# Second MLP: the normalised tile is turned in 32x32 blocks on VectorE and by DMA through DRAM instead of on TensorE

## The chip, the cores and the metric

One core of a Trainium2 chip. The metric is the device time of one execution in microseconds; a kernel's time is the median of its runs. A core has TensorE (PE, with its weight loads shown as PEld), VectorE (DVE), ScalarE (ACT), GpSimd (POOL) and SyncE (SP), whose queue issues nearly all DMAs here.

## What is computed

Memory attention, then two MLPs over 4352 tokens of 512 features (`S` = 512 tokens and 32 state rows for each of 8 batches). The change touches the second MLP alone:

```python
def _moe2_ref(x, w_in, w_out, g_ln):           # w_in 512 x 1024, w_out 1024 x 512
    h = x @ w_in
    e = np.exp(h - np.max(h, axis=-1, keepdims=True))
    sm = e / (np.sum(e, axis=-1, keepdims=True) + 1e-09)
    solu = h * sm
    mu = np.mean(solu, axis=-1, keepdims=True)
    var = np.mean((solu - mu) ** 2, axis=-1, keepdims=True)
    ln = (solu - mu) / np.sqrt(var + 1e-06) * g_ln
    return (ln @ w_out).astype(np.float32)
```

All matrix products keep nearly full f32 precision: each operand is split into a high part (fp32r) and the rest, and three products of the parts are summed.

## The kernel before

The first MLP writes its output, turned so that features lie on partitions, to DRAM (`x2_d`), a tensor for each block of 512 tokens and one of 256 state rows. The second MLP goes over 34 tiles of 128 tokens, four to a block and two for the state rows. A tile passes through these steps:

- `up` (line 731): 24 matmuls of 128x512, h = x W_in, into two banks of PSUM. There are two such pairs of banks (`ps_2`), used in turn, so tile s + 2 needs what tile s gave back.
- `solu_norm` (line 750): on VectorE a reduce for the maximum (752), on ScalarE the exponent with its sum (756), on VectorE the reciprocal (758) and the product with h (760), which is the last reader of the PSUM of h; on ScalarE the squares (764), on GpSimd the power -1/2 (766), on VectorE the final scale (767). The result is e, 128 tokens by 1024 features; `g_ln` is already in the weights.
- `trans` (line 770): eight TensorE transposes of 128x128 (777) into two banks, each bank then split by `split` (line 118): ScalarE copies the high part lh (119), VectorE subtracts to get ll (120).
- `down` (line 781): 24 matmuls (788 to 790) with blocks of lh and ll as the stationary operand, a copy to `ob` (801) and the store to the output (803, for state rows 808).

The loop runs over s: `up` of tile s, `down` of tile s - 2, `trans` of tile s - 1, `solu_norm` of tile s. At the end the last tile is transposed in the middle of the `down` before it. Beside this, `load_x2` (706) loads the next block from DRAM in two halves of 512 KB on SP's queue (271), and `split_x2` (714) splits them by the same `split`. In this part of the kernel the order of instructions on each engine is set by a planner from costs that it assumes; on the chip each engine takes its queue in order. Waits of DMAs stand in SP's queue and hold what is behind them.

Of the kernel before, what the change touches and what calls it, by code (L numbers as in the profile page):

```python
# [8 lines left out]
F32 = mybir.dt.float32  # L9
F32R = mybir.dt.float32r  # L10
# [10 lines left out]
def memory_attention_relu2_solu(  # L21
# [15 lines left out]
    nc = tc.nc  # L37
    P = 128
    B, H, S, D = x.shape
# [3 lines left out]
    F2 = w2_in.shape[1]  # L43
# [9 lines left out]
    NSR = B * NS  # L53
    scale = 1.0 / float(D) ** 0.5

    dram = ctx.enter_context(tc.tile_pool(name="dram", bufs=1, space=DRAM))
# [6 lines left out]
        dram.tile([P, NM, S if b < B else NSR], F32, name=f"x2_d{b}", tag=f"x2_{b}") for b in range(B + 1)  # L63
    ]

    x2p_d = [dram.tile([P, NM, S], F32, name=f"x2p_d{b}", tag=f"x2p_{b}") for b in range(2)]

    def pool(name, bufs, stack=ctx, **kw):
        return stack.enter_context(tc.tile_pool(name=name, bufs=bufs, reuse_waits="tile", **kw))
# [9 lines left out]
    swp = pool("swp", 4)  # L79
    stgp = pool("stgp", 4)  # L80
    cvp = pool("cvp", 2)
    a1p = pool("a1p", 2)
# [35 lines left out]
    def split(hi, lo, src):  # L118
        nc.scalar.activation(out=hi, in_=src, func=AF.Copy)
        nc.vector.tensor_tensor(out=lo, in0=src, in1=hi.bitcast(F32), op=ALU.subtract)  # L120
# [148 lines left out]
    def fetch32(src):  # L269
        t = stgp.tile([P, 2, 512], F32, tag="stg", name="st32")  # L270
        nc.sync.dma_start(out=t, in_=src)
        return t
# [427 lines left out]
    NK = F2 // P  # L700
# [3 lines left out]
    x2_st = {}  # L704

    def load_x2(blk):
        if blk < B:
            x2_st[blk] = [fetch32(x2_d[blk][:, 2 * i : 2 * i + 2, :]) for i in range(2)]
        else:
            t = stgp.tile([P, NM, NSR], F32, tag="stg", name="st_x2")  # L710
            nc.sync.dma_start(out=t, in_=x2_d[blk])
            x2_st[blk] = [t]

    def split_x2(blk):

        n = S if blk < B else NSR
        if blk not in x2_t:
            x2_t[blk] = (
                pools["x"].tile([P, NM, n], F32R, tag="x2h", name="x2h"),
                pools["x"].tile([P, NM, n], F32R, tag="x2l", name="x2l"),  # L720
                [],
            )
        hi, lo, at = x2_t[blk]
        st = x2_st[blk].pop(0)
        k0, nk = len(at), st.shape[1]
        at.extend(range(nk))
        split(hi[:, k0 : k0 + nk, :], lo[:, k0 : k0 + nk, :], st)
# [3 lines left out]
    def up(s, blk, t):  # L731
        xh, xl, _ = x2_t[blk]
        ps = ps_2[s % 2].tile([P, F2], F32, tag="h2", name="h2")
        for k in range(NM):
            for lt, hl in ((xh, (0, 1)), (xl, (0,))):
                for i in hl:
                    for a in range(2):
                        nc.tensor.matmul(  # L738
                            out=ps[:, a * 512 : (a + 1) * 512],
                            lhsT=lt[:, k, t * P : (t + 1) * P],  # L740
                            rhs=w2[k][:, i, a * 512 : (a + 1) * 512],
                            start=(k == 0 and lt is xh and i == 0),
                            stop=(k == NM - 1 and lt is xl),
                        )
        return ps

    def small(name):
        return pools["s"].tile([P, 1], F32, tag=name, name=name)

    def solu_norm(ps):  # L750
        nm = small("nm")
        nc.vector.tensor_reduce(out=nm, in_=ps, axis=AX.X, op=ALU.max)  # L752
        nc.vector.tensor_scalar_mul(nm, nm, -1.0)  # L753
        e = up_.tile([P, F2], F32, tag="u", name="e")
        sm = small("s2")
        nc.scalar.activation(out=e, in_=ps, func=AF.Exp, bias=nm, accum_out=sm)  # L756
        nc.vector.tensor_scalar_add(sm, sm, 1e-9)
        nc.vector.reciprocal(out=sm, in_=sm)
        mu = small("mu")
        nc.vector.scalar_tensor_tensor(out=e, in0=e, scalar=sm, in1=ps, op0=ALU.mult, op1=ALU.mult, accum_out=mu)  # L760
        nc.vector.tensor_scalar_mul(mu, mu, -1.0 / F2)  # L761
        j = evp.tile([P, F2], F32, tag="ev", name="j")
        var = small("var")
        nc.scalar.activation(out=j, in_=e, func=AF.Square, bias=mu, accum_out=var)  # L764
        nc.vector.tensor_scalar(out=var, in0=var, scalar1=1.0 / F2, scalar2=1e-6, op0=ALU.mult, op1=ALU.add)
        nc.gpsimd.tensor_tensor(out=var, in0=var, in1=mhalf, op=ALU.pow)
        nc.vector.tensor_scalar(out=e, in0=e, scalar1=mu, scalar2=var, op0=ALU.add, op1=ALU.mult)
        return e

    def trans(ln):  # L770
        lh = swp.tile([P, F2], F32R, tag="sw", name="lh")
        ll = swp.tile([P, F2], F32R, tag="sw", name="ll")
        for a in range(2):
            ps = pools["t"].tile([P, 512], F32, tag=f"t{a}", name="ps_t")
            for k in range(4):
                o = (4 * a + k) * P
                nc.tensor.transpose(ps[:, k * P : (k + 1) * P], ln[:, o : o + P], ident)  # L777
            split(lh[:, a * 512 : (a + 1) * 512], ll[:, a * 512 : (a + 1) * 512], ps)
        return lh, ll

    def down(blk, t, lh, ll, final):

        ps = pools["o"].tile([P, DM], F32, tag="o", name="ps_o")
        for k in range(NK):
            wt = w2[NM + k // 2]
            o = (k % 2) * 512
            a, bb = lh[:, k * P : (k + 1) * P], ll[:, k * P : (k + 1) * P]
            nc.tensor.matmul(out=ps, lhsT=a, rhs=wt[:, 0, o : o + 512], start=(k == 0), stop=False)  # L788
            nc.tensor.matmul(out=ps, lhsT=a, rhs=wt[:, 1, o : o + 512], start=False, stop=False)  # L789
            nc.tensor.matmul(out=ps, lhsT=bb, rhs=wt[:, 0, o : o + 512], start=False, stop=(k == NK - 1))  # L790
            yield k + 1
        ob = gp.tile([P, DM], F32, tag="gh", name="ob")
        if final:

            to = out[blk * SO : blk * SO + S].rearrange("(p t) e -> p t e", t=NT)[:, t, :]
            nc.scalar.activation(out=ob[:, : DM // 2], in_=ps[:, : DM // 2], func=AF.Copy)
            nc.vector.tensor_copy(out=ob[:, DM // 2 :], in_=ps[:, DM // 2 :])
            nc.scalar.dma_start(out=to[:, : DM // 2], in_=ob[:, : DM // 2])
            nc.sync.dma_start(out=to[:, DM // 2 :], in_=ob[:, DM // 2 :])
            return  # L800
        nc.scalar.activation(out=ob, in_=ps, func=AF.Copy)
        if blk < B:
            nc.sync.dma_start(out=out[blk * SO : blk * SO + S].rearrange("(p t) e -> p t e", t=NT)[:, t, :], in_=ob)
        else:
            per = P // NS
            for bb in range(per):
                b = t * per + bb
                nc.sync.dma_start(out=out[b * SO + S : (b + 1) * SO], in_=ob[bb * NS : (bb + 1) * NS, :])
# [30 lines left out]
    hid, sq, ready, left = {}, {}, {}, {}  # L839
# [66 lines left out]
    for s, (b, f) in enumerate(items):  # L906
# [9 lines left out]
        if g % 5 == 2 and 0 <= g // 5 + 1 < 16:  # L916
            n = g // 5 + 1
# [37 lines left out]
        n = S if b < B else NSR  # L955
# [12 lines left out]
        for e in ends.get(b, ())[1:]:  # L968
            i = f - e + 3
# [3 lines left out]
        sw = next((u for k, u in units.get(s - 2, []) if k == "i"), None)  # L973
# [26 lines left out]
    tiles = [(blk, t) for blk in [*range(B - 1), B, B - 1] for t in range(NT if blk < B else NSR // P)]  # L1000
    order = [blk for blk, t in tiles if t == 0]
# [3 lines left out]
    up_q = [solu_norm(up(0, *tiles[0]))]  # L1005
# [5 lines left out]
    ps_2[1] = pool("ps_2b", 1, space=PSUM)  # L1011
    pools["t"] = pool("ps_t", 1, space=PSUM)
    pools["o"] = pool("ps_o", 2, space=PSUM)
    ln_q = []
    for s in range(1, len(tiles) + 2):
        if s == 1:
            reload_w2(7, 1)
        if s < len(tiles):
            blk, t = tiles[s]
            i = order.index(blk) + 1  # L1020
            if i < len(order):
                if t == 0:
                    load_x2(order[i])
                if t >= 1 and x2_st[order[i]]:
                    split_x2(order[i])
                    if blk == B:
                        split_x2(order[i])
            ps = up(s, blk, t)
        if s == len(tiles) - 1:

            ln_q.append(trans(up_q.pop(0)))
        if s >= 2:
            lh, ll = ln_q.pop(0)
            for part in down(*tiles[s - 2], lh, ll, s == len(tiles) + 1):
                if s == len(tiles) and part == NK // 2:
                    ln_q.append(trans(up_q.pop(0)))
        if 1 <= s < len(tiles) - 1:
            ln_q.append(trans(up_q.pop(0)))
        if s < len(tiles):
            up_q.append(solu_norm(ps))  # L1040


# [28 lines left out]
```

## Time and profile before

| | before |
|---|---|
| median of 3 runs | 1117.78 us (1117.42 to 1118.10) |
| profiled execution, span | 1115.4 us |
| TensorE busy | 1096.8 us, 98% |
| VectorE busy | 708.5 us, 64% |
| ScalarE busy | 512.4 us, 46% |
| even part of the second MLP | 757.43 to 1075.31 us of the span, 27 tiles |

The span runs from the first to the last instruction; the time of a run lies 2.4 us above it. A timeline row gives the start from the beginning of the span, the duration, the engine, the line of the kernel, the operation, what is written and read, and in brackets the idle time before it with what ended it. Matmuls are pipelined: a row's duration is longer than the distance to the next one, so distances are read from starts.

### The profile page before, as it was taken

Reading aid. Unit: us, or ns where it says so; the run is one execution under the profiler, and the core shown is the slowest. Engines: PE = TensorE matmul, PEld = TensorE weight load, DVE = VectorE, ACT = ScalarE, POOL = GpSimd, SP = SyncE. Lnnn points to the kernel's source line nnn. Section 1 sums busy time; section 2 is a strip of 40 time slices with the busy share of each in tenths; the row PEclk is TensorE's granted clock in tenths of the full one; section 3 lists DMA queues with packets and bytes.
Section 4 is the critical chain, followed back from the end, with each engine's and each line's share of the span. In section 5 each row is a group of like instructions: output and inputs, shape, how many; then the busy total and the mean of one; then the engine's idle time right before and its main releaser. Section 6 shows DMA issues by size and latency. Waiting matters only on the chain.

```text
span 1115.4 us, 15150 instructions
## 1 busy us (share of the span) xinstructions
PE 1096.8 (98%) x5692; PEld 911.2 (82%) x5692; DVE 708.5 (64%) x1358; ACT 512.4 (46%) x903; POOL 44.7 (4%) x62
## 2 busy tenths in 40 slices
PE   5899999999999999999999999999999999999998
PEld 4788888888888888888888889888888888888887
DVE  7999995687686695884755446664545545455443
ACT  6899776455454452442333113343433334234232
POOL 1000000010000000000000000000000000000000
PEclk9899999999999999999999999999999999999999
DMA  9779883767766632412112027410101101000001
GB/s 275 253 229 311 273 276 85 239 199 221 215 198 181 200 130 69 149 62 79 40 38 76 25 91 263 151 57 20 67 19 58 67 20 41 26 20 29 20 19 38
DMA packets 93017, 134.69 MB, mean 121 GB/s; under 512 B 44816, under 2 KB 45584, under 8 KB 92944
## 3 DMA queue, kind: packets, MB, share of 16 engines
q1 hardware_dynamic: 92224, 133.46, 37.2%
q8 instruction: 45, 0.74, 0.3%
q10 hardware_dynamic: 720, 0.26, 0.1%
q14 instruction: 28, 0.23, 0.1%
HBM read 83.37 MB, written 49.28 MB: 119 GB/s over the span
## 4 chain that ended last, share of the span: by engine, by line
PE 93%; DVE 4%; ACT 1%; DMA 1%; issue 0%; ACTq 0%; POOL 0%; DVEq 0%; POOLq 0%
PE h L738 16%; PE acc L144 11%; PE acc L145 11%; PE acc L146 11%; PE ps_h L144 6%; PE ps_h L145 6%; PE ps_h L146 6%; PE ps_o L790 6%; PE ps_o L789 6%; PE ps_o L788 6%; PE ps_t L777 3%; PE ps_sr L553 2%; PE ps_x L135 1%; PE ps_sw L388 1%; PE ps_sw L389 1%; PE ps_c L494 1%
## 5 line engine op out<-in xcount | busy, mean ns | idle before, releaser
L144 PE MATMUL acc<-gh,w1out 128*128 128x512 f32 (+1 forms) x576 | 219.0, 380 | 0.0
L146 PE MATMUL acc<-gh,w1out 128*128 128x512 f32 (+1 forms) x576 | 217.9, 378 | 0.0
L145 PE MATMUL acc<-gl,w1out 128*128 128x512 f32 (+1 forms) x576 | 217.8, 378 | 0.0
L738 PE MATMUL h<-w,x2h 128*128 128x512 f32 x544 | 148.6, 395 | 0.0
L618 ACT ACTIVATE r<-ps_h 128x512 f32<-128x512 f32 (+1 forms) x144 | 82.4, 572 | 141.1 <-PE ps_h L146 139.6
L620 DVE TENSOR_TENSOR r<-r,ps_h 128x512 f32<-128x512 f32 (+1 forms) x112 | 72.4, 647 | 89.7 <-ACT r L618 89.1
L146 PEld LDWEIGHTS acc<-gh,w1out 128*128 128x128 f32 x576 | 108.4, 188 | 20.6
L144 PEld LDWEIGHTS acc<-gh,w1out 128*128 128x128 f32 x576 | 108.4, 188 | 20.4 <-DVE ev_x L657 0.2
L145 PEld LDWEIGHTS acc<-gl,w1out 128*128 128x128 f32 x576 | 108.4, 188 | 19.9
L738 PEld LDWEIGHTS h<-w,x2h 128*128 128x128 f32 x544 | 99.6, 188 | 18.9
L144 PE MATMUL ps_h<-ah,sw 128*128 128x512 f32 x256 | 107.1, 418 | 0.0
L788 PE MATMUL ps_o<-w,lh 128*128 128x512 f32 x272 | 106.0, 390 | 0.0
L790 PE MATMUL ps_o<-w,ll 128*128 128x512 f32 x272 | 105.9, 390 | 0.0
L789 PE MATMUL ps_o<-w,lh 128*128 128x512 f32 x272 | 105.8, 389 | 0.0
L634 DVE TENSOR_TENSOR gl<-r,gh 128x512 fp32r<-128x512 f32 (+1 forms) x144 | 96.4, 669 | 11.7 <-ACT r L627 8.7
L756 ACT ACTIVATE e<-h,nm 128x1024 f32<-128x1024 f32 x34 | 38.0, 1117 | 138.8 <-DVE nm L753 138.8
L146 PE MATMUL ps_h<-ah,sw 128*128 128x512 f32 x256 | 100.9, 394 | 0.0
L145 PE MATMUL ps_h<-al,sw 128*128 128x512 f32 x256 | 100.6, 393 | 0.0
L752 DVE TENSOR_REDUCE nm<-h 128x1 f32<-128x1024 f32 x34 | 41.6, 1224 | 82.6 <-PE h L738 82.6
L738 PE MATMUL h<-w,x2l 128*128 128x512 f32 x272 | 83.8, 389 | 0.0
L764 ACT ACTIVATE j<-e,mu 128x1024 f32<-128x1024 f32 x34 | 39.1, 1151 | 54.3 <-DVE mu L761 50.3
L738 PEld LDWEIGHTS h<-w,x2l 128*128 128x128 f32 x272 | 51.1, 188 | 10.8
(173 smaller groups left out, 1723.4 us busy)
## 6 DMA issues: line engine op xcount, KB each, us to landing
stg<-sw_d SPq DMA_DIRECT2D x120, 128.0 KB, 3.1
sw_d<-ev_sw SPq DMA_DIRECT2D x28, 512.0 KB, 4.0
st<-in_moe_w_out_dram SPq DMA_DIRECT2D x24, 512.0 KB, 4.8
xs<-in_x_dram SPq DMA_DIRECT2D x32, 256.0 KB, 4.2
w1i_d<-w1in SPq DMA_DIRECT2D x16, 512.0 KB, 4.7
st<-in_moe_w_in_dram SPq DMA_DIRECT2D x16, 512.0 KB, 5.3
w1in<-w1i_d SPq DMA_DIRECT2D x32, 256.0 KB, 4.6
x_d<-ev_x SPq DMA_DIRECT2D x16, 512.0 KB, 2.7
```

The lines of the kernel that those rows point to most:

```text
L144: nc.tensor.matmul(out=ps, lhsT=lh, rhs=rh, start=first and i == 0, stop=False)
L145: nc.tensor.matmul(out=ps, lhsT=lh, rhs=rl, start=False, stop=False)
L146: nc.tensor.matmul(out=ps, lhsT=ll, rhs=rh, start=False, stop=last and i == n - 1)
L618: nc.scalar.activation(out=r, in_=ps, func=AF.Relu)
L620: nc.vector.tensor_tensor(out=r, in0=r, in1=ps, op=ALU.mult)
L634: nc.vector.tensor_tensor(out=gl, in0=r, in1=gh.bitcast(F32), op=ALU.subtract)
L738: nc.tensor.matmul(out=ps[:, a * 512 : (a + 1) * 512], lhsT=lt[:, k, t * P : (t + 1) * P], rhs=w2[k][:, i, a * 512 : (a + 1) * 512], start ...
L752: nc.vector.tensor_reduce(out=nm, in_=ps, axis=AX.X, op=ALU.max)
L764: nc.scalar.activation(out=j, in_=e, func=AF.Square, bias=mu, accum_out=var)
L788: nc.tensor.matmul(out=ps, lhsT=a, rhs=wt[:, 0, o : o + 512], start=(k == 0), stop=False)
L789: nc.tensor.matmul(out=ps, lhsT=a, rhs=wt[:, 1, o : o + 512], start=False, stop=False)
L790: nc.tensor.matmul(out=ps, lhsT=bb, rhs=wt[:, 0, o : o + 512], start=False, stop=(k == NK - 1))
```

## The change

`trans` is replaced for all tiles but the last two. `turn` transposes e on VectorE in 32x32 blocks into `sq` (a buffer with the tag "ah" that the first MLP used), stores `sq` to a DRAM tensor of its own (512 KB, each partition one run of 4 KB), and loads it back with four DMAs, one for each 32 target partitions, in runs of 1 KB, into `lt` (tag "al"). After that the features of a chunk lie on partitions. `parts` splits `lt` into lh and ll: one copy on ScalarE and one subtraction on VectorE, 128x1024 each, SBUF to SBUF. In the loop, step s runs `up` of tile s, `turn` of tile s - 1, `parts` of tile s - 2, `down` of tile s - 3 and `solu_norm` of tile s; `down` thus comes one tile later. The last two tiles are still transposed on TensorE: tile n - 2 in the last step, tile n - 1 in the middle of the `down` of tile n - 2.

```diff
+    ln_d = [
+        dram.tile([P, F2], F32, name=f"ln_d{i}", tag=f"ln{i}") for i in range((B * S + NSR) // P)
+    ]
...
+    def turn(s, ln):
+        sq = a1p.tile([P, 4, NK, 32], F32, tag="ah", name="ln_sq")
+        nc.vector.transpose(
+            out=sq.rearrange("p q k t -> p k q t"), in_=ln.rearrange("p (k q t) -> p k q t", k=NK, q=4)
+        )
+        nc.sync.dma_start(out=ln_d[s], in_=sq.rearrange("p q k t -> p (q k t)"))
+        at = ln_d[s].rearrange("(j r) (q c) -> q r j c", j=4, q=4)
+        lt = a1p.tile([P, 4, NK, 32], F32, tag="al", name="ln_t")
+        for q in range(4):
+            nc.sync.dma_start(
+                out=lt[32 * q : 32 * (q + 1)].rearrange("r j k t -> r j (k t)"), in_=at[q]
+            )
+        return lt
+
+    def parts(lt):
+        lh = swp.tile([P, F2], F32R, tag="sw", name="lh")
+        ll = swp.tile([P, F2], F32R, tag="sw", name="ll")
+        to = [a.rearrange("p (k j t) -> p k j t", k=NK, j=4) for a in (lh, ll)]
+        split(*to, lt.rearrange("p j k t -> p k j t"))
+        return lh, ll
...
-    for s in range(1, len(tiles) + 2):
+    for s in range(1, n):
...
-        if s == len(tiles) - 1:
-            ln_q.append(trans(up_q.pop(0)))
-        if s >= 2:
-            lh, ll = ln_q.pop(0)
-            for part in down(*tiles[s - 2], lh, ll, s == len(tiles) + 1):
-                if s == len(tiles) and part == NK // 2:
-                    ln_q.append(trans(up_q.pop(0)))
-        if 1 <= s < len(tiles) - 1:
-            ln_q.append(trans(up_q.pop(0)))
-        if s < len(tiles):
-            up_q.append(solu_norm(ps))
+        ps = up(s, blk, t)
+        lt_q[s - 1] = turn(s - 1, up_q.pop(0)) if s <= n - 2 else None
+        if s >= 2 and lt_q[s - 2] is not None:
+            ln_q[s - 2] = parts(lt_q.pop(s - 2))
+        if s == n - 1:
+            by_pe(n - 2)
+        if s >= 3:
+            for _ in finish(s - 3):
+                pass
+        up_q.append(solu_norm(ps))
+    for s in (n - 3, n - 2, n - 1):
+        for k in finish(s):
+            if s == n - 2 and k == NK // 2:
+                by_pe(n - 1)
```

`by_pe(s)` is `trans` of the oldest e, and `finish(s)` is `down` of tile s with its lh and ll.

## Rows read from the trace of the kernel before

**Rows 1.** The page: span, busy time of each engine, chain that ended last

```profile
span 1115.4 us, 15150 instructions
PE 1096.8 (98%) x5692; PEld 911.2 (82%) x5692; DVE 708.5 (64%) x1358; ACT 512.4 (46%) x903; POOL 44.7 (4%) x62
...
PE 93%; DVE 4%; ACT 1%; DMA 1%; issue 0%; ACTq 0%; POOL 0%; DVEq 0%; POOLq 0%
```

**Rows 2.** Windows: busy time of each engine over 27 tiles, granted clock, DMA share

```profile
757.43:1075.31 317.88, 317.88 (x1514) 265.59 (x1513) 155.62 (x308) 116.66 (x201) 14.82 (x27) 1.00 0.10 35
```

**Rows 3.** Timeline of TensorE: one tile of the even stretch

```profile
851.61 1.03 PE L777 MATMUL ps_t<-ident,e 128*128 128x128 f32 x8
852.40 1.17 PE L738 MATMUL h<-w,x2h 128*128 128x512 f32 x4
...
857.94 0.39 PE L788 MATMUL ps_o<-w,lh 128*128 128x512 f32 x1
...
863.39 1.03 PE L777 MATMUL ps_t<-ident,e 128*128 128x128 f32 x8
```

**Rows 4.** Timeline of VectorE: a tile without and a tile with x2 splits

```profile
869.91 1.22 DVE L752 TENSOR_REDUCE nm<-h 128x1 f32<-128x1024 f32 x1 [2.88 <-PE h L738]
...
876.80 0.81 DVE L767 TENSOR_SCALAR e<-e,mu,var 128x1024 f32<-128x1024 f32 x1 [0.73 <-POOL var L766]
877.53 1.28 DVE L120 TENSOR_TENSOR ll<-ps_t,lh 128x512 fp32r<-128x512 f32 x2
881.69 1.23 DVE L752 TENSOR_REDUCE nm<-h 128x1 f32<-128x1024 f32 x1 [2.88 <-PE h L738]
...
890.76 0.81 DVE L767 TENSOR_SCALAR e<-e,mu,var 128x1024 f32<-128x1024 f32 x1 [0.73 <-POOL var L766]
```

**Rows 5.** Groups by line and shape, 730 to 1100 us: busy, mean ns, idle before

```profile
L120 DVE TENSOR_TENSOR x2l<-st,x2h 128x1024 fp32r<-128x1024 f32 x12 | 14.5, 1215 | 0.0
L119 ACT ACTIVATE x2h<-st 128x1024 fp32r<-128x1024 f32 x12 | 12.1, 1051 | 23.4 <-PE h L738 23.4
...
L753 DVE TENSOR_SCALAR nm<-nm 128x1 f32<-128x1 f32 x32 | 4.9, 152 | 0.8
```

**Rows 6.** DMA issues: of the page (KB, landing), then lines 664 and 410

```profile
sw_d<-ev_sw SPq DMA_DIRECT2D x28, 512.0 KB, 4.0
...
L664 SPq DMA_DIRECT2D x_d<-ev_x x18: 319/338/430, 197.5 to 722.3; - x18
...
DMA to landing us min/median/max: 2.1/2.9/6.5
...
L410 SPq DMA_DIRECT2D stg<-sw_d x64: 538/592/1035, 309.7 to 558.2; - x64
...
DMA to landing us min/median/max: 2.6/2.9/7.0
```

**Rows 7.** Timelines of TensorE and VectorE where the second MLP starts

```profile
715.91 1.09 PE L738 MATMUL h<-w,x2h 128*128 128x512 f32 x4
...
721.38 1.07 PE L738 MATMUL h<-w,x2h 128*128 128x512 f32 x4
722.28 0.61 PE L738 MATMUL h<-w,x2l 128*128 128x512 f32 x2
723.42 1.06 PE L777 MATMUL ps_t<-ident,e 128*128 128x128 f32 x8 [0.53 <-DVE e L767]
...
722.46 0.81 DVE L767 TENSOR_SCALAR e<-e,mu,var 128x1024 f32<-128x1024 f32 x1 [0.41 <-POOL var L766]
...
726.69 1.28 DVE L760 SCALAR_TENSOR_TENSOR e<-e,s,h 128x1024 f32<-128x1024 f32 x1
```

**Rows 8.** Timelines around the splits of the next block's x2

```profile
739.95 2.01 ACT L119 ACTIVATE x2h<-st 128x1024 fp32r<-128x1024 f32 x2 [3.92 <-PE h L738]
...
742.75 1.22 DVE L120 TENSOR_TENSOR x2l<-st,x2h 128x1024 fp32r<-128x1024 f32 x1
...
746.44 1.17 PE L738 MATMUL h<-w,x2h 128*128 128x512 f32 x4
```

More of the change, by code (lines that the diff above doesn't have):

```diff
@@ L1013, in memory_attention_relu2_solu, with by_pe, finish @@
     pools["o"] = pool("ps_o", 2, space=PSUM)
-    ln_q = []
-    for s in range(1, len(tiles) + 2):
+    n = len(tiles)
+    lt_q, ln_q = {}, {}
+    def by_pe(s):
+        ln_q[s] = trans(up_q.pop(0))
+    def finish(s):
+        lh, ll = ln_q.pop(s)
+        yield from down(*tiles[s], lh, ll, s == n - 1)
+    for s in range(1, n):
         if s == 1:
             reload_w2(7, 1)
-        if s < len(tiles):
[L1019 to L1024, printed above, removed]
-                    split_x2(order[i])
-                    if blk == B:
-                        split_x2(order[i])
-            ps = up(s, blk, t)
-        if s == len(tiles) - 1:
-            ln_q.append(trans(up_q.pop(0)))
-        if s >= 2:
-            lh, ll = ln_q.pop(0)
-            for part in down(*tiles[s - 2], lh, ll, s == len(tiles) + 1):
-                if s == len(tiles) and part == NK // 2:
-                    ln_q.append(trans(up_q.pop(0)))
-        if 1 <= s < len(tiles) - 1:
-            ln_q.append(trans(up_q.pop(0)))
-        if s < len(tiles):
-            up_q.append(solu_norm(ps))
+        blk, t = tiles[s]
+        i = order.index(blk) + 1
+        if i < len(order):
+            if t == 0:
+                load_x2(order[i])
+            if t >= 1 and x2_st[order[i]]:
+                split_x2(order[i])
+                if blk == B:
+                    split_x2(order[i])
+        ps = up(s, blk, t)
[12 more added lines that the diff above has]
+                by_pe(n - 1)
 _INS = ["x", "state", "moe_w_in", "moe_w_out", "moe2_w_in", "moe2_w_out", "moe2_g_ln"]
```

## The prediction

> **What bounds the kernel now.** I read the page first. TensorE is busy 98% of the span and carries 93% of the chain that ended last [rows 1], so time comes out only where TensorE does less work or waits less. Next I took the stretch in which the second MLP runs evenly: 27 tiles lie between two transposes of the same kind, 317.88 us, 11.773 us a tile, TensorE busy for all of it at a granted clock of 1.00, which is 2.4 GHz; VectorE is busy 155.62 us, 5.76 us a tile, 49% [rows 2]. The reader is to see that no other engine is near its limit. Then one tile on TensorE's timeline [rows 3]: eight transposes at 851.61, the 24 matmuls of `up` from 852.40, the 24 of `down` from 857.94, the next transposes at 863.39. They follow each other without a gap. Last I read VectorE in the same stretch [rows 4], because it takes over the work: from one reduce over h to the end of e it needs 7.70 us (869.91 to 876.80 + 0.81), part of it waiting (0.73 us for GpSimd ahead of 876.80, for one), and the two subtractions that make ll end at 878.81, 8.90 us after the reduce began. A tile that also splits x2 takes 9.88 us (881.69 to 890.76 + 0.81) with its ll pair inside, 0.98 us more.
>
> **What is removed.** There are 34 tiles and so 34 groups of eight transposes; 32 go, the last two stay. The transposes hold TensorE from 851.61 to 852.40, 0.79 us, and the weights that follow cost a little more. From outside: 24 matmuls of `down` take 5.45 us (857.94 to 863.39), so 48 at that pace take 10.90 us, and 11.773 - 10.90 = 0.87 us a tile is what the transposes cost. With `up` at the pace of the one that has no transposes ahead of it (715.91 to 721.38, 5.47 us [rows 7]) it is 0.85 us. I take 0.87: 32 x 0.87 = 27.8 us, at the least 32 x 0.85 = 27.2 us. All of it is on the path, since TensorE has nothing else to wait for here. Each tile also loses its two copies and two subtractions out of PSUM; they lie beside TensorE and give back nothing.
>
> **What VectorE gets.** `turn` is one 128x1024 f32 transpose, SBUF to SBUF; the trace has none. The cheapest 128x1024 row is the scale of e, 0.81 us [rows 4]; the plain two-operand one is 1.215 us [rows 5]; if each of the 32 blocks of 32 columns paid what a 128x1 instruction pays (0.152 us [rows 5]), it would be 4.9 us. I take 1.22, the row of an elementwise pass that reads and writes the same amount. `parts` is one subtraction of 128x1024, 1.22 us, for a pair of 1.28 us [rows 4, 5], and one copy on ScalarE, 1.05 us [rows 5]. VectorE's busy time becomes 5.76 + 1.22 - 0.06 = 6.9 of 10.9 us. Taken strictly one after the other, waits included, a tile is 8.90 - 0.06 + 0.98/4 (one tile in four splits x2) = 9.09 us, plus 1.22 = 10.3 us. That is below 10.9 even if the planner fills no gap, so TensorE stays the bound, but 0.6 us is a thin cover.
>
> A rule of the Trainium skill speaks against the step. "VectorE: DVE Perf Modes", section "The three transpose paths" and the table of rules after it, prices a 128x128 VectorE transpose (bf16) at 311 ns against 390 ns on TensorE, and says to use TensorE for 128x128 where PSUM will do. Eight times 311 ns is an estimate of 2.5 us for `turn`, and by it the strict sum would be 11.6 us, above 10.9: nearly all the gain gone. No run here shows a VectorE transpose. I hold 1.22 the likelier, since one instruction pays its fixed cost once.
>
> **What the DMA queues get.** A tile adds five DMAs on SP's queue: one store of 512 KB, then four loads of 128 KB that land on 32 partitions each and must wait until the store has landed. Stores of 512 KB into sw_d land in a median of 4.0 us, those of line 664 in 2.9, between 2.1 and 6.5. Loads of just this shape, 128 KB onto 32 partitions, exist (line 410): SP spends 0.59 us on each, up to 1.04, and they land 2.9 us after issue, 2.6 to 7.0 [rows 6]. The round trip R is thus 4.0 + 3 x 0.59 + 2.9 = 8.7 us; 2.1 + 3 x 0.54 + 2.6 = 6.3 and 6.5 + 3 x 1.04 + 7.0 = 16.6 are the ends. While SP waits for the store, about 4 us a tile, the store of ob and the loads of x2 stand behind it. They have most of a tile in hand: ob has three buffers and leaves once a tile, and x2 is loaded a block ahead.
>
> **The wait that is added.** On VectorE the subtraction of `parts` waits for the loads, and if the planner keeps the order of the code, the reduce of a tile two further on stands behind it. That closes a loop over two tiles: reduce to e (7.70), `turn` (1.22), R, copy (1.05), subtraction (1.22) = 11.19 + R [rows 4 to 6]. Two tiles of TensorE are 21.8 us, so the loop is hidden while R stays under 10.6 us; with 8.7 there are 1.9 us to spare, which is the work that hides the DMAs. `down` itself has more: it runs one tile later, so its data may come about ten microseconds after they are there. A second cover also shrinks: the splits of x2 start when the last `up` of a block ends (739.95) and end at 743.97 (742.75 + 1.22), before the next block's `up`, which stood at 746.44 [rows 8]. Without the transposes that `up` comes 0.8 us sooner, so 1.7 us remain. I cost it at nothing; if `turn` slips into that gap, it may cost up to 1 us in each of 8 blocks.
>
> **The start.** The first `down` comes a tile later, so `up` of tiles 1, 2 and 3 run back to back. `up` of tile 2 would end at 721.38 + 5.47 = 726.85; that of tile 3 needs the PSUM of tile 1, free when the multiply at 726.69 ends, 727.97 [rows 7]: a stall of 1.1 us. It then ends at 733.4. e of tile 0 is there at 722.46 + 0.81 = 723.27; `turn`, R, copy and subtraction bring 723.27 + 1.22 + 8.7 + 1.05 + 1.22 = 735.5. The first `down` needs that half a microsecond after its start, so it starts near 735.0, a stall of 1.6 us. Against it goes the gap of 0.7 us by which the first transposes waited for e (722.28 + 0.45 to 723.42). Net 2.0 us; with `turn` queued behind the next reduce 3.2. I take 2.5; the ends are 0 (data early, the planner finds other work) and 10 (R of 16.6). At the end of the kernel the last two tiles are transposed as now, with one more `down` ahead of them, and nothing is gained or lost.
>
> **The sum.** The profiled execution has a span of 1115.4 us, 2.4 below the median of 1117.8; I take the difference as fixed. 1117.8 - 27.8 + 2.5 = 1092.5 us. Its own range goes from 1117.8 - 27.8 - 0.7 = 1089 to 1117.8 - 27.2 + 5 = 1096 us.
>
> **Rivals.** (A) VectorE becomes the bound. If `turn` costs T and the planner fills no gap, a tile is 9.09 + T; above T = 1.8 us it exceeds TensorE's 10.9. At T = 2.3 (0.152 plus twice 1.07, an element every second cycle) it is 11.4 us, which saves 0.38 x 32 = 12 us: 1108 us with the start; at T = 2.5, 11.6 us and 6 us saved, 1114 us; at T = 2.7 the gain is gone, 1118 us. Against it: VectorE's gaps are filled already, as by the x2 splits, of which the second begins at 742.75 while ScalarE turns to the exponent [rows 8], and with all gaps filled T could be almost 5 us. (B) The loop over the DMAs binds a little: R between 10.6 and 12.4. At 11.5 a tile is (11.19 + 11.5)/2 = 11.35 us, 0.42 x 32 = 13.5 us saved, 1107 us. For it: landings up to 6.5 and 7.0 us in [rows 6]. Against it: those belong to stages in which many transfers run at once; here the DMA engines are 10% busy [rows 2]. (C) Slower: the same loop with the four loads landing one behind the other instead of together. R = 4.0 + 4 x 2.9 = 15.6 us, a tile (11.19 + 15.6)/2 = 13.4 us, 1.63 x 32 = 52 us more than now, 1170 us; it is slower from R = 12.4 on. Against it: line 410 issues its four 0.59 us apart and each lands 2.9 us after its own issue, so they overlap. (D) The change removes the transposes but the planner puts the waits so that TensorE stands still for as long: about 1117 us.
>
> **How the numbers follow.** The forecast gets 0.78, A 0.08, B 0.06, C 0.05, D 0.03. A measurement of this kernel can tell some 0.2%, 2.2 us, from no change. Faster: 0.78 + 0.05 of A + 0.06 = 0.89; within 0.2%: 0.03 of A + 0.01 of D = 0.04; slower: 0.05 of C + 0.02 of D = 0.07. The range reaches from 1088 up into B and the mild part of A, to 1105, which leaves out somewhat under 0.2.
>
> **What would show it.** Right: 16 transposes on TensorE in place of 272, an even stretch of 10.9 us a tile with TensorE still without gaps, `turn` near 1.2 us, and the last of the four loads some 9 us after the store's issue; a gap of 1 to 4 us ahead of the first two or three groups after 726 us. Wrong: an idle TensorE in the even stretch, released by VectorE (A: VectorE without gaps; B and C: VectorE waiting for lt); or TensorE waiting for x2l once a block. The forecast falls if a tile of the even stretch takes over 11.1 us, or the start costs over 5 us.

## The result and the profile after

| | before | after |
|---|---|---|
| median | 1117.9 us | 1093.0 us (1092.1 to 1094.4, 4 runs) |
| ratio | | 0.9779, 95% interval 0.9765 to 0.9793 |
| profiled execution, span | 1115.4 us | 1090.9 us |
| TensorE, transposes in the second MLP | 272 | 16 |
| VectorE busy | 708.5 us | 743.4 us |

The change makes the kernel 2.2% faster. The page of the kernel after answers [rows 1]; the two DMA lines give name, engine queue, count, KB and us to landing:

```profile
span 1090.9 us, 14924 instructions
PE 1068.8 (98%) x5436; PEld 884.8 (81%) x5436; DVE 743.4 (68%) x1358; ACT 512.5 (47%) x871; POOL 44.7 (4%) x62
...
PE 92%; DVE 3%; DMA 2%; ACT 1%; SPq 1%; issue 1%; POOL 0%; DVEq 0%; ACTq 0%; POOLq 0%
...
ln_d<-ln_sq SPq DMA_DIRECT2D x32, 512.0 KB, 2.6
ln_t<-ln_d SPq DMA_DIRECT2D x128, 128.0 KB, 2.9
```

TensorE still sets the time. It is busy for 28 us less, and the span is 24.5 us shorter. The even stretch, by windows (length; busy time and instructions of PE, PEld, DVE, ACT, POOL; granted clock; DMA share; GB/s), and TensorE's timeline of one tile, the counterparts of [rows 2, 3]:

```profile
770.00:1050.00 280.00, 280.00 (x1237) 231.94 (x1236) 176.76 (x296) 113.85 (x168) 14.30 (x26) 1.00 0.41 137
...
883.96 1.07 PE L741 MATMUL h<-w,x2h 128*128 128x512 f32 x4
...
889.39 0.39 PE L813 MATMUL ps_o<-w,lh 128*128 128x512 f32 x1
...
894.84 1.07 PE L741 MATMUL h<-w,x2h 128*128 128x512 f32 x4
```

`up` now follows `down` directly, 894.84 - 883.96 = 10.88 us a tile where it was 11.77. TensorE has no gap from 752 us to the last `up`. The DMA engines went from 10% to 41% busy [rows 2], and the matmuls did not get slower: `down` took 5.45 us before [rows 3] and takes 894.84 - 889.39 = 5.45 us now.

VectorE and its group rows (count, busy, mean ns, idle before), the counterparts of [rows 4, 5]:

```profile
889.60 1.23 DVE L755 TENSOR_REDUCE nm<-h 128x1 f32<-128x1024 f32 x1 [1.91 <-PE h L741]
...
892.73 1.28 DVE L763 SCALAR_TENSOR_TENSOR e<-e,s,h 128x1024 f32<-128x1024 f32 x1
...
893.93 1.22 DVE L123 TENSOR_TENSOR ll<-ln_t,lh 128x1024 fp32r<-128x1024 f32 x1
...
898.53 1.25 DVE L787 STREAM_TRANSPOSE ln_sq<-e 128x1024 f32<-128x1024 f32 x1
900.48 1.23 DVE L755 TENSOR_REDUCE nm<-h 128x1 f32<-128x1024 f32 x1 [0.70 <-PE h L741]
```

```profile
L123 DVE TENSOR_TENSOR ll<-ln_t,lh 128x1024 fp32r<-128x1024 f32 x32 | 39.0, 1217 | 0.4
L787 DVE STREAM_TRANSPOSE ln_sq<-e 128x1024 f32<-128x1024 f32 x31 | 38.6, 1245 | 1.0
...
L122 ACT ACTIVATE lh<-ln_t 128x1024 fp32r<-128x1024 f32 x32 | 33.6, 1049 | 1.3 <-DMA ln_t<-ln_d 1.2 <-ACT j L767 0.2
```

The transpose takes 1.245 us. The planner put the subtraction of `parts` inside the chain of a later tile, right behind its product with h (893.93), where VectorE would have waited for ScalarE's squares. ScalarE waited for the loads 1.2 us in all. VectorE still stands idle for TensorE ahead of 21 of 27 reduces (1.91 and 0.70 us here), and TensorE has no gap, so VectorE is not the bound.

SP's queue (start, us, DMA, count) shows the round trip of one tile: the store at 887.72, the four loads when it has landed, issued within 1.74 us:

```profile
887.72 0.34 SPq L790 DMA_DIRECT2D ln_d<-ln_sq  x1
890.32 1.74 SPq L794 DMA_DIRECT2D ln_t<-ln_d  x4
895.66 0.36 SPq L828 DMA_DIRECT2D out_dram<-ob  x1
```

The time that came back at the start, from TensorE's timeline (compare [rows 7]) and VectorE's beside it:

```profile
716.15 1.09 PE L741 MATMUL h<-w,x2h 128*128 128x512 f32 x4
...
726.61 0.61 PE L741 MATMUL h<-w,x2l 128*128 128x512 f32 x2
728.98 1.16 PE L741 MATMUL h<-w,x2h 128*128 128x512 f32 x4 [1.76 <-DVE e L763]
...
734.08 0.61 PE L741 MATMUL h<-w,x2l 128*128 128x512 f32 x2
736.01 1.17 PE L741 MATMUL h<-w,x2h 128*128 128x512 f32 x4 [1.32 <-DVE e L763]
...
750.19 0.61 PE L741 MATMUL h<-w,x2h 128*128 128x512 f32 x2
751.44 0.50 PE L815 MATMUL ps_o<-w,ll 128*128 128x512 f32 x1 [0.64 <-DVE ll L123]
```

```profile
723.44 1.22 DVE L755 TENSOR_REDUCE nm<-h 128x1 f32<-128x1024 f32 x1
724.57 1.24 DVE L787 STREAM_TRANSPOSE ln_sq<-e 128x1024 f32<-128x1024 f32 x1
725.73 0.11 DVE L756 TENSOR_SCALAR nm<-nm 128x1 f32<-128x1 f32 x1
...
727.55 1.28 DVE L763 SCALAR_TENSOR_TENSOR e<-e,s,h 128x1024 f32<-128x1024 f32 x1
...
733.07 1.25 DVE L787 STREAM_TRANSPOSE ln_sq<-e 128x1024 f32<-128x1024 f32 x1
...
734.58 1.28 DVE L763 SCALAR_TENSOR_TENSOR e<-e,s,h 128x1024 f32<-128x1024 f32 x1
```

From the last start plus two matmuls (0.45 us) to the next start, the gaps are 1.92, 1.48 and 0.80 us, and about 0.1 us goes with the first group behind each: 4.5 us. The first two are `up` of tiles 3 and 4 waiting for the PSUM of tiles 1 and 2, which the product with h gives back late, because a transpose stands ahead of it on VectorE: for tile 1 between the reduce and nm (725.73), without which the exponent can't start, for tile 2 (733.07) right ahead of the product. The third is `down` of tile 1 waiting for ll.

### The profile page after: what moved, and what is told of

Read it like the earlier page. It is cut to its first block, busy times and chain, and to the rows that moved or that the text cites. A ratio compares the mean times of both kernels' runs of the same rounds, so it can differ in the third digit from the quotient of the medians.

```text
span 1090.9 us, 14924 instructions
## 1 busy us (share of the span) xinstructions
PE 1068.8 (98%) x5436; PEld 884.8 (81%) x5436; DVE 743.4 (68%) x1358; ACT 512.5 (47%) x871; POOL 44.7 (4%) x62
## 4 chain that ended last, share of the span: by engine, by line
PE 92%; DVE 3%; DMA 2%; ACT 1%; SPq 1%; issue 1%; POOL 0%; DVEq 0%; ACTq 0%; POOLq 0%
PE h L741 15%; PE acc L147 11%; PE acc L149 11%; PE acc L148 11%; PE ps_h L147 6%; PE ps_h L149 6%; PE ps_h L148 6%; PE ps_o L815 6%; PE ps_o L813 5%; PE ps_o L814 5%; PE ps_sr L556 2%; PE ps_x L138 1%; PE ps_sw L391 1%; PE ps_sw L392 1%; SPq L444 1%
## 5 line engine op out<-in xcount | busy, mean ns | idle before, releaser
L741 PE MATMUL h<-w,x2h 128*128 128x512 f32 x544 | 146.1, 389 | 3.1 <-DVE e L763 3.1
L741 PEld LDWEIGHTS h<-w,x2h 128*128 128x128 f32 x544 | 101.8, 188 | 24.8 <-issue 2.2
L637 DVE TENSOR_TENSOR gl<-r,gh 128x512 fp32r<-128x512 f32 (+1 forms) x144 | 96.4, 669 | 11.2 <-ACT r L630 8.0
L815 PEld LDWEIGHTS ps_o<-w,ll 128*128 128x128 f32 x272 | 51.0, 188 | 11.6 <-DVE ll L123 1.1
L814 PEld LDWEIGHTS ps_o<-w,lh 128*128 128x128 f32 x272 | 51.1, 188 | 10.6
```

The costliest lines, as they stand in the source:

```text
L637: nc.vector.tensor_tensor(out=gl, in0=r, in1=gh.bitcast(F32), op=ALU.subtract)
L741: nc.tensor.matmul(out=ps[:, a * 512 : (a + 1) * 512], lhsT=lt[:, k, t * P : (t + 1) * P], rhs=w2[k][:, i, a * 512 : (a + 1) * 512], start ...
```

## The experiments

Three questions were open: whether VectorE's price or the DMA round trip comes near to setting the time, what the later place of `down` is for, and where the microseconds of the start come from. Since a trace has the same 280 us for every kernel, the even stretch is compared by TensorE's instructions from 770 to 1050 us; 48 matmuls make a tile, so 1237 of them are 280 x 48 / 1237 = 10.87 us a tile. What is lost at the two ends shows in a second measure, from the `up` of tile 1 to the last matmul (starts, us). It leaves out what differs ahead of the second MLP, which alone sets the two executions of the changed kernel 3.1 us apart:

| kernel | `up` of tile 1 | last matmul | between |
|---|---|---|---|
| before | 715.91 | 1111.32 | 395.4 |
| changed; second run | 716.15; 719.27 | 1086.81; 1089.95 | 370.7; 370.7 |
| two transposes | 717.78 | 1091.75 | 374.0 |
| one more step; with `ob` on ScalarE | 717.75; 717.95 | 1107.48; 1094.50 | 389.7; 376.6 |
| `down` back; `down` later alone | 716.44; 715.30 | 1093.87; 1111.99 | 377.4; 396.7 |
| tile 0 on TensorE; second run | 716.38; 717.71 | 1084.73; 1086.01 | 368.4; 368.3 |
| and the last tile but one turned | 717.46 | 1086.28 | 368.8 |

### VectorE's price: the transpose twice and four times

```diff
-        nc.vector.transpose(
+        for _ in range(2):          # and 4
+            nc.vector.transpose(
```

> The changed kernel with the 32x32 transpose of each turned tile issued twice, so that VectorE spends 2.49 us a tile on it instead of 1.245 (the price that eight times the 311 ns of the Trainium skill would give). Theory (the planner lays VectorE's added work into the gaps of the chain from reduce to e): VectorE's busy time goes from 6.85 to 8.1 us a tile, below TensorE's 10.88, so the even stretch stays at 10.88 us a tile and the time at 1093 to 1096 us, the rest being a longer start. Rival A of the prediction (strictly one after the other): 9.09 + 2.49 = 11.58 us a tile, 0.70 x 32 = 22 us more, 1115 us.

Measured: 1097.1 us, ratio to before 0.9809 (0.9793 to 0.9826).

> The same with the transpose issued four times, 4.98 us a tile. VectorE's busy time becomes 6.85 + 3.74 = 10.6 us a tile, just under TensorE's 10.88. Theory (gaps filled as far as they go): some waits for ScalarE and GpSimd can't be filled, so VectorE becomes the bound at 11 to 12.5 us a tile, 1097 to 1145 us. Rival A (strict order): 9.09 + 4.98 = 14.07 us a tile, 3.19 x 32 = 102 us more, 1195 us.

Measured: 1114.6 us, one run. Windows of the kernel with two, then with four transposes:

```profile
770.00:1050.00 280.00, 280.00 (x1236) 231.67 (x1235) 209.35 (x319) 113.10 (x167) 14.25 (x26) 1.00 0.39 134
```

```profile
770.00:1050.00 280.00, 275.45 (x1192) 221.34 (x1191) 247.59 (x358) 108.66 (x159) 13.70 (x25) 1.00 0.38 131
```

At twice the price the even stretch is untouched, 1236 instructions against 1237: rival A in its strict form is out, since it gave 1115 us. At four times VectorE is busy 88% and a tile takes 280 x 48 / 1192 = 11.28 us, 0.4 us more, far from the strict 14.07. What two transposes cost, they cost at the start: `up` of tile 4 now waits until 739.72, a gap of 3.56 us, and from the seventh matmul behind it on they run slower for about 3 us. TensorE's timeline and windows of the kernel with two transposes:

```profile
735.71 0.62 PE L741 MATMUL h<-w,x2l 128*128 128x512 f32 x2
739.72 1.17 PE L741 MATMUL h<-w,x2h 128*128 128x512 f32 x4 [3.39 <-DVE nm L756]
...
742.85 0.63 PE L814 MATMUL ps_o<-w,lh 128*128 128x512 f32 x1
743.28 0.63 PE L815 MATMUL ps_o<-w,lh 128*128 128x512 f32 x1
```

```profile
739.70:744.00 4.30, 4.28 (x13) 3.47 (x14) 3.86 (x8) 3.28 (x5) 0.55 (x1) 0.67 0.44 150
```

The starts from 742.85 on are 0.43 us apart instead of 0.23, and the granted clock of the stretch is 0.67: part of it ran at the lower level, 1.2 GHz.

### The round trip: one and two more steps through DRAM

```diff
         nc.sync.dma_start(out=ln_d[s], in_=sq.rearrange("p q k t -> p (q k t)"))
+        nc.sync.dma_start(out=ln_h0[s], in_=ln_d[s])
...
-        at = ln_d[s].rearrange("(j r) (q c) -> q r j c", j=4, q=4)
+        at = ln_h0[s].rearrange("(j r) (q c) -> q r j c", j=4, q=4)
```

> The changed kernel with one more step on the way through DRAM: after the store has landed, SP copies the tile from DRAM to a second DRAM tensor, 512 KB, and the four loads read that. The round trip R goes from about 6.9 us (store 2.6, three issues of 0.43, load 2.9) to about 10. The prediction's loop (11.19 + R over two tiles of 10.88) hides R up to 10.6: 1093 to 1096 us, with some 3 us more at the start at most. Rival (a thinner cover than that, the loop binds already): (11.19 + 12)/2 = 11.6 us a tile, 1116 us.

Measured: 1113.4 us, ratio 0.9955 (0.9940 to 0.9970).

> The same with two more steps, R about 13 us. The prediction's loop, in which the reduce of a tile two further on stands behind the subtraction that waits for the loads: (11.19 + 13.2)/2 = 12.2 us a tile, 1.3 x 32 = 42 us more, 1135 us. Rival (the planner has put that subtraction behind the multiply with h, so that the reduce doesn't wait; the loop is then only copy, squares, scale, turn and R, some 5.6 + R, hidden up to R of 16): the even stretch stays at 10.88 us, 1093 to 1099 us. Third possibility: SP's queue, which waits out each step in order, is taken for 2.6 + 2 x 3.2 + 1.7 = 10.7 us a tile and becomes the bound once a step takes over 3.3 us: with 4.5 us a step 13.3 us a tile, 1170 us.

Measured: 1149.5 us, one run, which none of the three possibilities gave. DMA lines of the kernel with one more step, from 760 to 1060 us:

```profile
ln_t<-ln_h SPq DMA_DIRECT2D x108, 128.0 KB, 3.7
ln_h<-ln_d SPq DMA_DIRECT2D x26, 512.0 KB, 5.2
ln_d<-ln_sq SPq DMA_DIRECT2D x26, 512.0 KB, 3.6
```

and, over the whole of the same kernel, the longest wait of SP's queue (total us, times, longest):

```profile
SPq L832 <- ACT ob L830: 134.1, 21, 12.1
```

The step costs 5.2 us, more than the 3 expected, and the others land later too: R = 3.6 + 5.2 + 1.3 + 3.7 = 13.8 us. So the test went past the prediction's limit of 10.6, and its loop would give (11.19 + 13.8)/2 = 12.5 us a tile. The even stretch of that kernel, by windows:

```profile
770.00:1050.00 280.00, 277.22 (x1199) 222.77 (x1198) 168.55 (x280) 107.95 (x157) 13.16 (x24) 1.00 0.57 180
```

280 x 48 / 1199 = 11.2 us. Both expectations for the time missed, the cheap one with a step priced too low, the dear one, which came within 3 us, with a loop that does not bind in that way: it puts 11.6 us on a tile. The waits name another suspect: SP stands still for `ob`, whose copy comes at the end of a `down`, and steps stand behind it. (The changed kernel has this wait too, 92.4 us, and no gap on TensorE in the even stretch.) Hence the next two kernels: the same, with the stores of `ob` issued by ScalarE.

```diff
-            nc.sync.dma_start(out=out[blk * SO : blk * SO + S]...[:, t, :], in_=ob)
+            nc.scalar.dma_start(out=out[blk * SO : blk * SO + S]...[:, t, :], in_=ob)
```

> The kernel with one more step through DRAM, and the store of ob issued by ScalarE instead of SP. With the extra step alone the time was 1113.4 us: store 3.4, step 5.0, loads 3.6 us to landing, so R is about 13.3 us, and SP waited 134 us for ob, with the extra step and the loads queued behind it. Theory (what the longer way costs comes from SP's queue, where a store that waits for the end of a down holds the loads behind it): with ob gone from SP's queue the gaps of the even stretch (8.8 us from 760 to 1040 us) and most of the 8 us at the end go, 1096 to 1103 us. Rival (R itself is too long for the cover): 1110 to 1114 us as before.

Measured: 1099.6 us, ratio 0.9837 (0.9823 to 0.9850), 13.8 us less than with `ob` on SP's queue. Its even stretch, by windows:

```profile
770.00:1050.00 280.00, 279.50 (x1227) 229.29 (x1227) 172.24 (x283) 111.20 (x160) 13.75 (x25) 1.00 0.57 185
```

280 x 48 / 1227 = 10.95 us a tile, so a way of R = 2.9 + 4.6 + 1.3 + 3.6 = 12.4 us is hidden almost wholly in the even stretch. That SP's queue made the data late is not shown, though the expectation came true. The planner laid out the other engines anew as well: between 803 and 813 us ScalarE runs lh, j, lh, `ob` in the one kernel and j, `ob`, lh in the other. And with `ob` on SP ScalarE did not wait for a load once: loads land 2.4 to 5.1 us after issue there, and for every tile but the last the copy begins over 5.1 us after the last of its four loads was issued. What TensorE waited for is the place of copies and subtractions in their engines' queues. The edit changes both, that order and SP's queue, and which of them gave back the time stays open. With `ob` on ScalarE, where the time is shorter, there is even a little waiting for loads (ScalarE's waits from 722 to 1098 us):

```profile
ACT lh L125 <- DMA ln_t<-ln_h: 3.4, 2, 2.8
```

> The same with two more steps, R about 20 us of landings; with ob on SP's queue 1149.5 us, with single gaps of 4 to 7 us in which TensorE waited for lh. Theory (SP's queue): the large gaps go, 1100 to 1120 us. Rival (R itself): 1140 us and more.

Measured: 1138.7 us, one run, 11 us less than with `ob` on SP, and near the rival's 1140. With two more steps most of the loss stays, but late: from 770 to 980 us 915 matmuls run, 210 x 48 / 915 = 11.0 us a tile, with R = 5.6 + 5.8 + 4.8 + 1.3 + 2.9 = 20.4 us. Behind that TensorE waits for lh, as in this line of its timeline, with ScalarE's rows beside it:

```profile
988.31 0.80 PE L821 MATMUL ps_o<-w,lh 128*128 128x512 f32 x1 [3.75 <-ACT lh L128]
```

```profile
984.37 0.60 ACT L834 ACTIVATE ob<-ps_o 128x512 f32<-128x512 f32 x1 [4.01 <-PE ps_o L823]
...
987.21 1.04 ACT L128 ACTIVATE lh<-ln_t 128x1024 fp32r<-128x1024 f32 x1
```

The copy stands in ScalarE's queue behind `ob`, which waits for a `down`, and behind an exponent that waited for VectorE. Its four loads had been issued by 973.5, and loads of this kernel land 2.4 to 5.2 us after issue: the data lay there for 8 us and more. At TensorE's other gaps of over 2 us ahead of lh the copy begins 5.3 to 15.2 us after the last load was issued. So these waits are the order that the planner chose for the longer way and not R, and the rival came near the time without its cause.

### The later down, taken back and alone

```diff
-        if s >= 3:
-            for _ in finish(s - 3):
+        if s >= 2:
+            for _ in finish(s - 2):
```

> The changed kernel with the matmuls down moved back to where they were, a tile earlier (down of tile s - 2 in step s). Theory: the data of a tile are there 1.25 + 6.9 + 1.05 + 1.22 = 10.4 us after its e, and down would ask for them 13.9 us after it, so the even stretch holds at 10.88 us a tile; the first down waits longer, up to 8 us against 4.2 us of gaps now, so 1093 to 1098 us. Rival (the later place of down is what makes the turn through DRAM possible): TensorE waits for lt in every tile, 1 to 4 us, 1125 us and more.

Measured: 1099.8 us, ratio 0.9833 (0.9818 to 0.9849). Its even stretch by windows, then TensorE's timeline at the end of the kernel:

```profile
770.00:1050.00 280.00, 279.84 (x1230) 229.17 (x1230) 173.72 (x288) 112.32 (x163) 13.74 (x25) 1.00 0.39 134
```

```profile
1071.80 0.27 PE L780 MATMUL ps_t<-ident,e 128*128 128x128 f32 x1
1074.95 0.61 PE L813 MATMUL ps_o<-w,lh 128*128 128x512 f32 x1 [2.88 <-ACT lh L122]
1075.36 0.63 PE L814 MATMUL ps_o<-w,lh 128*128 128x512 f32 x1
```

The theory holds for the stretch, 10.93 us a tile, but not for the ends: 6.8 us are lost, most of them at the end of the kernel. At the start, where it looked for the loss, the same three gaps stand as in the changed kernel (1.76, 1.34 and 0.65 us idle for 1.76, 1.32 and 0.64). At the end lh of the last turned tile waits on ScalarE behind the exponent of the last tile. TensorE stands idle 3.05 us, and the matmuls behind it are 0.41 to 0.43 us apart. The later `down` is cover for the end of the kernel, not a condition of the way through DRAM.

The other part alone keeps all transposes on TensorE and moves only `down`:

```diff
-        lt_q[s - 1] = turn(s - 1, up_q.pop(0)) if s <= n - 2 else None
-        if s >= 2 and lt_q[s - 2] is not None:
-            ln_q[s - 2] = parts(lt_q.pop(s - 2))
+        if s <= n - 2:
+            by_pe(s - 1)
```

> The other part alone: all tiles transposed on TensorE as before, but down one tile later, so that three up run back to back at the start. Theory (the first two gaps of the changed kernel, 1.9 and 1.5 us, are up waiting for the PSUM of the tile two before it, and come from the place of down, not from the turn): 1118 us plus 1 to 3 us, 1119 to 1121 us. Rival (the gaps come from VectorE's transposes standing ahead of the multiply with h): no more than 1118.5 us.

Measured: 1119.0 us against 1118.1 us, ratio 1.0006 (0.9997 to 1.0015), not clear of no change and at the lower edge of what the theory expected. Its trace has two new gaps of 0.61 us at the start, 1.2 us together, and the second MLP is 1.3 us longer. So the place of `down` alone costs about a third of the net 3.8 us that the start costs in the changed kernel. It does not follow that it is a third of them there: with the turn, the start is the same whether `down` is written early or late. What the turn brings is the transposes ahead of the product with h; how the 3.8 us divide is not shown.

### Tile 0 on TensorE

```diff
+        if s == 1:
+            by_pe(0)
-        lt_q[s - 1] = turn(s - 1, up_q.pop(0)) if s <= n - 2 else None
+        lt_q[s - 1] = turn(s - 1, up_q.pop(0)) if 2 <= s <= n - 2 else None
...
-        if s >= 3:
-            for _ in finish(s - 3):
+        if s == 2 or s >= 4:
+            for _ in finish(0 if s == 2 else s - 3):
```

> The changed kernel with tile 0 transposed on TensorE and its down a tile earlier than the others, so that a down stands between up of tile 2 and of tile 3. Theory: the three gaps of the start go (1.92 + 1.48 + 0.80 and 0.3 us of slow groups behind them, 4.5 us), and eight transposes (0.89 us) with their wait for e (0.7 us as in the kernel before) come back: 1093.0 - 4.5 + 1.6 = 1090.1 us. Rival (the gaps only move to the pair up of tiles 3 and 4 that now stand next to each other): 1092 to 1094 us.

Measured: 1091.2 us (1090.9 to 1091.9), ratio 0.9760 (0.9747 to 0.9773). This kernel and the changed one ran once more side by side:

> The changed kernel itself, beside the next one on the same chip: 1093 us.

> The kernel with tile 0 on TensorE, against the changed kernel on the same chip. Theory (3.0 us of gaps fewer at the start, net of the transposes that come back): 1.5 to 2 us less than the changed kernel, 1091 us. Rival (the difference seen between two calls, 1091.2 and 1093.0, was the chip's): equal within 0.5 us.

Measured: 1094.3 us (ratio 0.9788, 0.9775 to 0.9802) and 1091.2 us (0.9763, 0.9750 to 0.9777). The two intervals just touch; the medians differ by 1.7 us in the first pair and by 3.1 us in the second. The traces are plainer: the second MLP is 2.3 and 2.4 us shorter. The three gaps have gone but for one of 0.15 us idle, and the wait of the first transposes for e is back (0.52). TensorE's timeline of the kernel with tile 0 on TensorE (second run), with what each row waited for:

```profile
724.09 0.61 PE L741 MATMUL h<-w,x2l 128*128 128x512 f32 x2
...
725.23 1.06 PE L780 MATMUL ps_t<-ident,e 128*128 128x128 f32 x8 [0.52 <-DVE e L770]
...
760.63 0.50 PE L815 MATMUL ps_o<-w,ll 128*128 128x512 f32 x1 [0.15 <-DVE nm L756]
```

The last tile but one was then turned through DRAM as well:

> The kernel with tile 0 on TensorE, and the last tile but one turned through DRAM as well, so that only the first and the last tile are transposed on TensorE. Two downs stand between its e and its own down, so the round trip of 10.4 us has 10.9 us of cover and more. Theory: another 0.89 us less, 1089.2 us. Rival (its parts come late at the end and TensorE waits): no gain or 1 to 3 us lost against the kernel with tile 0 on TensorE alone.

Measured: 1091.9 us (ratio 0.9762, 0.9749 to 0.9776): nothing gained. ScalarE's and TensorE's timelines at the end show the rival's case:

```profile
1073.55 0.60 ACT L826 ACTIVATE ob<-ps_o 128x512 f32<-128x512 f32 x1 [4.43 <-PE ps_o L815]
1074.05 1.05 ACT L122 ACTIVATE lh<-ln_t 128x1024 fp32r<-128x1024 f32 x1
```

```profile
1075.15 0.50 PE L813 MATMUL ps_o<-w,lh 128*128 128x512 f32 x1 [0.76 <-ACT lh L122]
```

The four loads were issued from 1064.64 to 1066.4 and landed a median of 2.7 us later, about 1069; the copy that reads them stands behind the copy of `ob`, which waits for a `down`. A gap of 1.0 us takes the place of 0.89 us of transposes. Tile 0 on TensorE alone is the fastest kernel found.

## Why the prediction was right, step by step

Predicted were 1092.5 us, measured 1093.0 us. The mechanism held; that the sum came within 0.5 us is partly luck, for two terms were off against each other, by 0.8 and 1.3 us.

- **The transposes.** 0.87 us a tile was the forecast; 11.773 - 10.88 = 0.89 us came off, 28.6 us in all against 27.8. The 0.02 us between the two are `up`, which takes 889.39 - 883.96 = 5.43 us now, a little less than the 5.45 of `down` that the working used for both. Nothing took the place of the transposes in the even stretch.
- **The start.** 2.5 us was taken; 4.5 us of gaps less the 0.7 of before are 3.8 us. The forecast had the mechanism of the first gap, PSUM of tile 1, with 1.1 us for 1.92. `turn` queued behind the next reduce, the condition of its worse case (3.2 us net), is what the planner did; but that case delays the first `down`, while the transpose delayed nm and so the PSUM of tile 1. It named the wrong cause for the second gap: not data late for the first `down`, but PSUM of tile 2 for the next `up`, which the planner had moved ahead of that `down`. The data of tile 0 were in fact later than forecast, 740.6 for 735.5, but this `up` covered it. The third it did not have. 28.6 - 3.8 = 24.8 us; the span lost 24.5, for the second MLP began 0.24 us later (`up` of tile 1 at 716.15 against 715.91 [rows 7]).
- **VectorE.** `turn` was 1.245 us for an assumed 1.22, `parts` 1.217 for 1.22, the copy 1.049 for 1.05 [rows 5], and busy time a tile 176.76 x 10.87 / 280 = 6.9 us as forecast. By the estimate from the Trainium skill ("VectorE: DVE Perf Modes", section "The three transpose paths": 311 ns for 128x128 in bf16, eight times 2.5 us) it would have been twice that; the trace does not agree for one instruction of 128x1024 f32. The fear behind rival A, a strict sum of 10.3 us with 0.6 to spare, was too dark: with a price of 2.49 us the even stretch still held, because the planner fills the gaps. The other end, T of almost 5 us, was too bright: at 4.98 a tile takes 11.28 us.
- **The round trip.** R is 2.6 + 3 x 0.43 + 2.9 = 6.8 us against 8.7: the store lands sooner than into sw_d [rows 6], and SP issues a load in 0.43 us where line 410 took 0.59. The limit of 10.6 us from the loop was not the right rule: at 13.8 us a tile took 11.2 us, not 12.5, and 10.95 at 12.4 with `ob` on ScalarE. Its condition, that the planner keeps the order of the code, did not hold: the subtraction stands behind a product with h. What was underrated is that order: with a longer way TensorE waited for copies and subtractions whose data, but for a few tiles, had landed.
- **The x2 splits.** Costed at nothing, and no gap shows at a block's end.
- **Rivals.** A, B and C did not happen; D neither, since TensorE has no gap in the stretch.

## What to carry to other kernels

When one engine is busy all the time, work moved to idle engines is worth what it occupied on the busy one, and that is read from the period of the even stretch, not from the durations of the rows. What it costs sits at the ends, where the lead that hides the longer way has to be built up and run down: handle the first piece the old way, and look at which queue holds the first consumer. Where TensorE waits for data that came by DMA, compare when the load landed with when its reader got to it: in the kernels with a longer round trip ScalarE waited for loads 0 to 8.6 us in all, while the second MLP grew by 6 to 56 us.

## What the runs showed of the hardware

- A 32x32 block transpose of 128x1024 f32 on VectorE takes 1.245 us, the price of an elementwise pass over as many elements (1.217 us).
- A copy of 512 KB from DRAM to DRAM took 4.6 to 5.8 us to landing (medians of the four kernels with such steps), a store of the same size from SBUF 2.6 us in the changed kernel and 2.9 to 5.7 us in these four.
- Idle TensorE of 1.76 us left the granted clock at its upper level (1.00 from 729 to 731 us of the changed kernel). Behind the gap of 3.05 us the first matmuls started 0.41 to 0.43 us apart where 0.23 is the pace at the upper level (granted clock 0.57 from 1074.9 to 1077 us); behind that of 3.56 us six kept the pace before the clock fell. Shorter gaps close together did it too: in the kernel with one more step 1.57 and 0.70 us idle, ahead of 1078.06 and 1079.49, and then a granted clock of 0.50 from 1079.4 to 1082 us.
- With the DMA engines 41% busy instead of 10%, matmuls kept their pace, 24 in 5.45 us.
